# A token-mixing kernel on one core: the filter's way back on quarters of the array, rows exchanged by DMA, six w1 parts made in the first stage and seven low parts by accumulating DMA

## The chip, the cores and the metric

The kernel runs on one core of a Trainium2 chip. The metric is the device time of one execution in microseconds (us); before the change the median of three runs is 391.92 us (391.39 to 392.2). A core has several engines that each work through a queue of their own, in order, and wait for one another through semaphores: TensorE (in the profile PE, its loading of stationary operands PEld), VectorE (DVE), ScalarE (ACT) and GpSimd (POOL). SyncE (SP) computes nothing here; it issues transfers. Sixteen DMA engines carry what SP and POOL issue. Operands lie in SBUF, 128 partitions (rows) wide; TensorE writes to PSUM, which has eight banks, each 512 fp32 columns wide.

## The reference

The input `x` is (1, 2048, 512). Two branches start from its layer norm and meet in a product:

```python
xn = _layernorm(x, axis=-1)
X = rfft2(xn) * (w_r + 1j * w_i)
s = irfft2(X, s=(2048, 512))
h = _layernorm(xn, axis=-1)
u = gelu(einsum("bsd,sf->bdf", h, w1) + b1)
y = einsum("bdf,fs->bds", u, w2) + b2
return x + s * silu(y.transpose(0, 2, 1))
```

`w1` is 2048 x 1792, `w2` is 1792 x 2048. The first branch is a filter in the two-dimensional spectrum, the second an MLP over the tokens.

## The kernel before

The 2048 tokens lie as 128 partitions times 16 blocks `j`. The 1792 hidden features are 14 tiles of 128 (`ft`). Large products run in fp32r with both operands split into a high and a low part, as three matmuls into one bank (`mm3`, lines 121 to 124). The transforms run in plain fp32; the trace shows two matmul records and two weight loads for each such matmul.

**First stage.** For each block `j`: layer norm, seven hidden tiles accumulated in banks 0 to 6 (`hidden_early`, line 333), the first transform of the spectrum into bank 7 (line 212), a copy and a fold into the tile `ey`. The raw `w1` parts of a block are split into high (`high`, ACT, line 325) and low (`low`, DVE, line 328). ACT and DVE instructions of this stage are kept in program order.

**Filter stage.** Two things run interleaved. One is the other seven hidden tiles for all 16 blocks, 112 calls of `hidden` (through `mm3`, so the trace shows them at lines 122 to 124). Their `w1` is fetched in 32 parts, 16 of four tiles each (512 columns, two SP transfers) and 16 of three tiles (384 columns), and split by `w1_part`, three parts ahead; high by ACT, low by DVE, both at line 119. The other is the filter, eight pairs `n` of `filter_pair`:

1. two blocks of four full-array matmuls (line 446), each copied from PSUM to `sh` by ACT;
2. eight matmuls of 64 rows x 32 columns (line 455), two signal halves into banks 5 and 4;
3. for each of two items (`filtered`): ACT makes `zt`, the signal with its upper and lower 64 partitions exchanged (lines 475 and 476); DVE forms sums and differences (lines 484 to 487), multiplies with the weights `wt` (line 493), adds (494), and forms `pq` (498) and `r` (499); ACT brings `r` into `pq` with exchanged halves (503 and 504);
4. the way back: four full-array matmuls an item, `pq` against the constant `hf`, into bank 3 (line 525), copied to `ey` by ACT (line 527).

In between come the gelus (`gelu`, ACT) and the forms of `u` that the last stage needs (`forms`, line 273 and 292 to 295, ACT and DVE). They need tiles of a pool of 25, of which 16 hold the normed input and come free as the hidden tiles pass. A loop over `steps` writes out the order of the filter's steps and paces the hidden tiles evenly between them; a scheduler then orders each engine's instructions for itself.

**Last stage.** Eight pairs of output blocks: `w2` loaded, combined and split (lines 633 to 645), seven products for each pair (line 766), the channel transform (line 701) and the gate. Its first weights share memory with the filter's tiles, which are given back at the end of the filter stage.

Of the kernel before, what the change touches and what calls it, by code (L numbers as in the profile page):

```python
# [22 lines left out]
NS = 25  # L23
WARM = 16
TAIL = 2
# [18 lines left out]
def _constants():  # L44
# [27 lines left out]

    g = np.zeros((P, 8, 2, 2, 32))
    back = np.zeros((8, 2, P, P))
    freq = np.zeros((P, 8, 2), int)
    j = np.arange(16)
    for lo in range(16):
        for hi in range(4):
            k1, (n, l), (t, h) = 16 * hi + lo, divmod(lo, 2), divmod(hi, 2)
            for r in range(16):  # L80
# [7 lines left out]
                elif r == 0:  # L88
                    k = [0, S // 2]
                    out[0, cr], out[1, cr] = 1.0, np.cos(np.pi * j)  # L90
                else:
                    k = [128 * r if r < 8 else 64 + 128 * (r - 8)] * 2
                    th = 2 * np.pi * ((j * k[0]) % S) / S
                    out[0, rows[r >= 8]], out[1, rows[r >= 8]] = np.cos(th), -np.sin(th)
                for s in range(2):
                    p, rows = 64 * s + l * 32 + h * 16 + r, slice(64 * t, 64 * t + 64)
                    g[rows, n, l, s, h * 16 + r] = back[n, t, p, l * 64:l * 64 + 64] = out[s, rows]
                    freq[p, n, t] = k[s]
# [7 lines left out]
        "c_h": back.reshape(16, P, P).astype(np.float32),  # L106
    }
    return c, freq


def spectral_mixer_kernel(tc, x, w1, b1, w2, b2, wk, we, wx, c_f, c_ft, c_d, c_i, c_g, c_h, out):
# [14 lines left out]
    with tc.tile_pool(name="ps", bufs=1, space=PSUM) as psp, ExitStack() as left, ExitStack() as right:  # L126
# [7 lines left out]
        pad = pers.tile([P, 1], F32, name="pad")  # L134
        G.memset(pad, 0.0)
# [4 lines left out]
        hup = pool(left, "left", "hu", NS)  # L140

        def new_hu(name):
            return hup.tile([P, 2, D], F32R, name=name, tag="hu")
# [131 lines left out]
        def held_tile(name):  # L275
            held[0] += 1
            return new_hu(name)
# [26 lines left out]
        def form_parts(n, i):  # L304
            t, k = form[i][n]
            return t[:, k, :D // 2], t[:, k, D // 2:]

# [57 lines left out]
        for j in range(NJ):  # L365
# [3 lines left out]
            if j == 0:  # L369
# [3 lines left out]
                SY.dma_start(b2t, b2)  # L373
            if j == 4:
# [36 lines left out]
            if more:  # L411
                low(w[1][1], raws[j + 1, 1], w[1][0])
                if not early:
# [6 lines left out]
            folds = fold(j, first_copy(j, z))  # L420
        run(folds)
# [10 lines left out]
        G.tensor_sub(e2[:, :, 1], wet[:, :, 1, 1, 1], wet[:, :, 0, 1, 1])  # L432

# [3 lines left out]
        def filter_pair(n):  # L437
# [4 lines left out]
            sh = []  # L442
            for l in range(2):
                pd = ps[:, 6]
# [3 lines left out]
                A.activation(sh[l], pd, AF.Copy)  # L448
                yield

            for s in range(2):
                for l in range(2):
                    for t in range(2):
                        rows, to = slice(64 * t, 64 * t + 64), 64 * s + 32 * l
                        T.matmul(ps[to:to + 32, (5, 4)[t]], gf[rows, l, s], sh[l][rows], start=True, stop=True)  # L455
            items = [filtered(n, t) for t in range(2)]
            for t in (0, 1, 0):
                next(items[t])
            yield
# [5 lines left out]

        def filtered(n, t):

            i = lo = 2 * n + t
            wt = mp.tile([P, 4, 256], F32, name=f"wt{i}", tag="wt")
            SY.dma_start(wt, wk[:, i])  # L470
            hf = mp.tile([P, P], F32, name=f"hf{i}", tag="hf", bufs=3)
            SY.dma_start(hf, c_h[i])
            px = ps[:, (5, 4)[t]]
            zt = mp.tile([P, D], F32, name=f"zi{lo}", tag="zi")
            A.activation(zt[:64], px[64:], AF.Copy, scale=-1.0)
            A.activation(zt[64:], px[:64], AF.Copy)

            def parts(a):
                v = a.rearrange("p (g s c) -> p s g c", s=2, c=64)
                return v[:, 0], v[:, 1]  # L480

            (pr, pi), (tr, ti) = parts(px), parts(zt)
            xc = mp.tile([P, 4, 4, 64], F32, name=f"xc{lo}", tag="xc")
            V.tensor_add(xc[:, 0], pr, ti)
# [3 lines left out]
            s1 = mp.tile([P, 2, 2], F32, name=f"s1_{lo}", tag="s1")  # L488
# [339 lines left out]
```

## Time and profile before

| what | before |
|---|---|
| median of three runs | 391.92 us |
| the profiled execution, its own time | 391.48 us |
| its span, first to last instruction | 389.7 us |
| mean granted TensorE clock | 0.999 |
| first stage | 0 to 98.44 us |
| filter stage | 98.44 to 217.29 us |
| last stage | 217.29 to 389.7 us |
| w1 loads in the filter stage | 36 of 128 KB, 16 of 64 KB, on SP |
| weights of the filter, wt | 16 of 512 KB, on SP |

The stage borders are the start of the first matmul of line 122 and of line 766. In lists of groups the columns are: line, engine, operation, operands, shapes and count, then busy time and mean duration of one (ns), then idle time of that engine just before, with what ended it. Timeline rows give start, duration and operation, with the idle time before in brackets. In the chain of work each piece counts from the point at which the one before it let it go, so pieces add up. A matmul's recorded duration includes the way through the array, so that neighbours overlap; the distance from start to start tells what one costs.

### The profile page before, as it was taken

Reading aid. Unit: us, or ns where it says so; the run is one execution under the profiler, and the core shown is the slowest. Engines: PE = TensorE matmul, PEld = TensorE weight load, DVE = VectorE, ACT = ScalarE, POOL = GpSimd, SP = SyncE. Lnnn points to the kernel's source line nnn. Section 1 sums busy time; section 2 is a strip of 40 time slices with the busy share of each in tenths; the row PEclk is TensorE's granted clock in tenths of the full one; section 3 lists DMA queues with packets and bytes.
Section 4 is the critical chain, followed back from the end, with each engine's and each line's share of the span. In section 5 each row is a group of like instructions: output and inputs, shape, how many; then the busy total and the mean of one; then the engine's idle time right before and its main releaser. Section 6 shows DMA issues by size and latency. Waiting matters only on the chain.

```text
span 389.7 us, 7277 instructions
## 1 busy us (share of the span) xinstructions
PE 380.7 (98%) x2552; PEld 333.8 (86%) x2552; DVE 325.8 (84%) x776; ACT 247.3 (63%) x455; POOL 58.2 (15%) x108
## 2 busy tenths in 40 slices
PE   8999999999999999999989989999999999999995
PEld 4888888888778777887778989999999999999995
DVE  5899998866599999978998699797978788787874
ACT  4676765664878864688748595565656464656442
POOL 2133332321100000000000002120202011110200
PEclk9999999999999999999999999999999999999999
DMA  8957457213725546545617659888868788695602
GB/s 264 325 162 249 136 190 256 69 50 90 218 72 157 170 128 202 150 116 172 195 42 254 135 181 224 197 205 172 227 135 227 148 219 164 197 153 170 110 7 54
DMA packets 33929, 64.21 MB, mean 165 GB/s; under 512 B 4066, under 2 KB 18274, under 8 KB 33764
## 3 DMA queue, kind: packets, MB, share of 16 engines
q1 hardware_dynamic: 29284, 52.33, 42.2%
q0 software_dynamic: 4608, 11.41, 17.7%
q8 instruction: 20, 0.33, 0.3%
q14 instruction: 17, 0.14, 0.1%
HBM read 59.53 MB, written 8.13 MB: 174 GB/s over the span
## 4 chain that ended last, share of the span: by engine, by line
PE 77%; DVE 7%; DMA 7%; ACT 5%; issue 3%; SPq 1%; POOL 0%; DVEq 0%; ACTq 0%; POOLq 0%
PE ps L766 27%; PE ps L333 20%; PE ps L123 5%; PE ps L122 5%; PE ps L124 5%; PE ps L212 4%; PE ps L446 4%; DMA s<-in_w_dram 3%; PE ps L701 3%; PE ps L525 2%; PE ps L455 2%; DMA out_dram<-g 2%; PE ps L322 2%; DVE w2f L645 1%; DMA a<-in_w_dram 1%
## 5 line engine op out<-in xcount | busy, mean ns | idle before, releaser
L333 PE MATMUL ps<-h,w1h 128*128 128x512 f32 x224 | 58.5, 398 | 0.0
L645 DVE TENSOR_TENSOR w2f<-s,w2f 128x896 fp32r<-128x896 f32 x32 | 34.9, 1092 | 18.8 <-ACT w2f L644 18.0
L333 PEld LDWEIGHTS ps<-h,w1h 128*128 128x128 f32 x224 | 40.9, 188 | 7.9
L122 PE MATMUL ps<-h,w1h 128*128 128x512 f32 x112 | 47.1, 422 | 0.0
L124 PE MATMUL ps<-h,w1l 128*128 128x512 f32 x112 | 44.1, 394 | 0.0
L123 PE MATMUL ps<-h,w1h 128*128 128x512 f32 x112 | 43.9, 392 | 0.0
L766 PE MATMUL ps<-fa,w2f 128*128 128x256 f32 x336 | 43.3, 282 | 0.0
L766 PE MATMUL ps<-fc,w2f 128*128 128x256 f32 x336 | 41.7, 280 | 1.1 <-DVE fc L273 1.1
L766 PE MATMUL ps<-fb,w2f 128*128 128x256 f32 x336 | 42.6, 281 | 0.1
L766 PEld LDWEIGHTS ps<-fa,w2f 128*128 128x128 f32 x336 | 41.4, 188 | 0.9 <-DVE w2f L645 0.2
L766 PEld LDWEIGHTS ps<-fc,w2f 128*128 128x128 f32 x336 | 40.2, 188 | 1.7 <-DVE fc L273 1.5
L766 PEld LDWEIGHTS ps<-fb,w2f 128*128 128x128 f32 x336 | 40.7, 188 | 0.7 <-DVE c L736 0.5
L644 ACT ACTIVATE w2f<-s 128x896 fp32r<-128x896 f32 x32 | 30.1, 948 | 16.4 <-DVE s L658 11.3
L635 POOL DMA_DIRECT2D s<-in_w_dram x16 | 13.8, 862 | 120.3 <-DVE tt L709 52.6
L645 DVE TENSOR_TENSOR w2f<-a,w2f 128x896 fp32r<-128x896 f32 x24 | 26.0, 1085 | 5.6 <-ACT w2f L644 5.6
L333 PE MATMUL ps<-h,w1l 128*128 128x512 f32 x112 | 30.6, 390 | 0.0
L122 PEld LDWEIGHTS ps<-h,w1h 128*128 128x128 f32 x112 | 21.2, 189 | 9.9 <-issue 6.7
L644 ACT ACTIVATE w2f<-a 128x896 fp32r<-128x896 f32 x24 | 22.8, 948 | 10.6 <-PE ps L766 7.4
L124 PEld LDWEIGHTS ps<-h,w1l 128*128 128x128 f32 x112 | 21.0, 188 | 4.9 <-DVE w1l L119 0.2
L333 PEld LDWEIGHTS ps<-h,w1l 128*128 128x128 f32 x112 | 21.0, 188 | 4.5
L123 PEld LDWEIGHTS ps<-h,w1h 128*128 128x128 f32 x112 | 21.2, 189 | 3.1
L217 ACT ACTIVATE zt<-ps 128x512 f32<-128x512 f32 x16 | 9.6, 597 | 21.6 <-PE ps L212 21.4
(125 smaller groups left out, 784.1 us busy)
## 6 DMA issues: line engine op xcount, KB each, us to landing
a<-in_w_dram SPq DMA_DIRECT2D x24, 448.0 KB, 3.6
wt<-in_wk_dram SPq DMA_DIRECT2D x16, 512.0 KB, 3.7
s<-in_w_dram SPq DMA_DIRECT2D x16, 448.0 KB, 4.3
s<-in_w_dram POOLq DMA_DIRECT2D x16, 448.0 KB, 6.6
w1s<-in_w_dram SPq DMA_DIRECT2D x48, 128.0 KB, 2.6
w1r<-in_w_dram SPq DMA_DIRECT2D x16, 256.0 KB, 3.6
x<-in_x_dram SPq DMA_DIRECT2D x15, 256.0 KB, 3.3
out_dram<-in_x_dram SPq DMA_DIRECT2D x4, 960.0 KB, 6.6
```

What stands on the lines that cost most here:

```text
L122: T.matmul(o, lh, rh, start=first, stop=False)
L123: T.matmul(o, lh, rl, start=False, stop=False)
L124: T.matmul(o, ll, rh, start=False, stop=last)
L212: T.matmul(z[:, b], h[:, b * P:(b + 1) * P], c, start=True, stop=True)
L217: keep(A.activation(zt, z, AF.Copy))
L333: T.matmul(ps[:, bank + i], w[wi][:, i * P:(i + 1) * P], hj, start=first and j == 0, stop=last and j == NJ - 1)
L446: T.matmul(pd[:, b * P:(b + 1) * P], eyl(2 * n + l)[:, b], cd[:, b], start=True, stop=True)
L635: G.dma_start(t, w2_half(*added), accum_op=ALU.add)
L644: A.activation(wf[:, 0], v, AF.Copy)
L645: V.tensor_sub(wf[:, 1], v, wf[:, 0].bitcast(F32))
L701: T.matmul(pe[:, b % 2, b // 2], yt[:, b], ci[:, b], start=True, stop=True)
L766: T.matmul(o, wf[:, wi, i], ui, start=m + a == 0 and n in (1, 2, 5), stop=m == NH - 1 and a == 2, skip_group_check=n in (6, 3, 7, 4))
```

## The change

The way back becomes matmuls of 64 rows by 64 columns: for each pair `n`, item `t`, block `b`, half `l` and signal part `s` one, each on the quarter (`l`, `s`) of the array, with 64 moving columns, into banks 3 and 4. The signal parts of one frequency now lie 32 partitions apart within a half, and `zt` is no longer made by two ACT copies: ACT makes one copy `px`, and four SP transfers of 32 partitions each exchange its rows into `zt`. DVE forms sums and differences in two operations with a sign taken from the column `turn`, and `pq` comes straight from two more. The real rows of the first item take their weights by four small POOL transfers. The loads `wt` go from SP to POOL's queue.

The first six `w1` parts are loaded, and split by ACT and DVE, in blocks 6 to 11 of the first stage, into six of nine early tiles of the same 25. Of the other 26 parts, seven (10, 12, ... 22) get their low part from an ACT copy with negative sign, to which two POOL transfers add `w1`. Three gelus move ahead of the filter stage. The order of filter steps, form steps and hidden tiles is written out in `PACE`, `MADE` and `LAST`; step 6 of a pair, the way back, stands directly ahead of the forward block of the pair two later. TensorE's instructions of this stage are kept in program order.

```diff
+NV = 9
+NE = 6
+FIRST = 6
+START = 4
+PACE = [(2, 2, 2, 1, 1, 1)] * 4 + [(2, 2, 2, 2, 1, 1)] * 4
+LAST = (4, 4, 4, 4, 4)
+MADE = (3, 3, 3, 3, 3, 3, 2, 2)
+ADDED = range(10, 24, 2)
...
+        def w1_runs(i, where, queue, **how):
+            f = 0
+            for f0, nf in BATCHES[i // NJ][0]:
+                queue.dma_start(where[:, f:f + nf * P], w1[:, i % NJ, f0 * P:(f0 + nf) * P], **how)
+                f += nf * P
+
+        def w1_early_load(i):
+            if i % 2 == 0:
+                pairs[i // 2] = usp.tile([P, 2, D], F32, name=f"w1e{i}", tag="u")
+            w1_runs(i, pairs[i // 2][:, i % 2], SY)
...
+            if FIRST <= j + 1 < FIRST + NE:
+                w1_early_load(j + 1 - FIRST)
...
+                if FIRST <= j < FIRST + NE:
+                    i = j - FIRST
+                    w1_early[i] = new_hu(f"w1e{i}", True)
+                    high(w1_early[i][:, 0], pairs[i // 2][:, i % 2])
+                    low(w1_early[i][:, 1], pairs[i // 2][:, i % 2], w1_early[i][:, 0])
...
+            if i in ADDED:
+                A.activation(wh, w, AF.Copy)
+                A.activation(wl, wh.bitcast(F32), AF.Copy, scale=-1.0)
+                w1_runs(i, wl, G, accum_op=ALU.add)
+                return wh, wl
+            split(wh, wl, w)
...
+        T = Kept(T, keep)
+        w1_parts = [w1_part(0)]
+        for ft, bank in ((2, 2), (0, 0), (1, 1)):
+            next(folds)
+            gelu(ft, bank)
...
-                pd = ps[:, 6]
+                pd = ps[:, 6 - l]
...
-                        rows, to = slice(64 * t, 64 * t + 64), 64 * s + 32 * l
-                        T.matmul(ps[to:to + 32, (5, 4)[t]], gf[rows, l, s], sh[l][rows], start=True, stop=True)
+                        rows, to = slice(64 * t, 64 * t + 64), 64 * l + 32 * s
+                        T.matmul(ps[to:to + 32, 6 - t], gf[rows, l, s], sh[l][rows], start=True, stop=True)
...
+            po = [ps[:, bank].rearrange("p (b t c) -> p b t c", b=4, t=2) for bank in (3, 4)]
+            for t, (pq, hf) in enumerate(((pq0, hf0), (pq1, hf1))):
+                for b in range(4):
+                    for s in range(2):
+                        for l in range(2):
+                            rows = slice(64 * l, 64 * l + 64)
+                            T.matmul(po[l][64 * s:64 * s + 64, b, t], pq[rows, b, s], hf[rows, s], start=True, stop=True)
+            for l in range(2):
+                A.activation(eyl(2 * n + l), po[l].rearrange("p b t c -> p b (t c)"), AF.Copy)
...
-            SY.dma_start(wt, wk[:, i])
+            G.dma_start(wt, wk[:, i])
+            yield
+            px = mp.tile([P, 2, 256], F32, name=f"px{i}", tag="px", bufs=3)
+            A.activation(px[:, ::-1].rearrange("p s (g c) -> p g s c", c=64),
+                         ps[:, 6 - t].rearrange("p (g s c) -> p g s c", s=2, c=64), AF.Copy)
...
+            for to, of in ((0, 32), (32, 0), (64, 96), (96, 64)):
+                SY.dma_start(zt[to:to + 32], px[of:of + 32])
...
-            A.activation(zt[:64], px[64:], AF.Copy, scale=-1.0)
-            A.activation(zt[64:], px[:64], AF.Copy)
...
-            V.tensor_add(xc[:, 0], pr, ti)
-            V.tensor_sub(xc[:, 1], pr, ti)
-            V.tensor_sub(xc[:, 2], tr, pi)
-            V.scalar_tensor_tensor(xc[:, 3], tr, -1.0, pi, op0=ALU.mult, op1=ALU.subtract)
...
+            for k, to in enumerate((xv[:, 0::3], zt)):
+                V.scalar_tensor_tensor(to, zt, turn[:, k:k + 1], px[:, ::-1], op0=ALU.mult, op1=ALU.add)
             V.tensor_mul(xv, xv, wt)
-            V.tensor_add(xv[:, 0:2], xv[:, 0:2], xv[:, 2:4])
+            V.tensor_sub(xv[:, 0:2], xv[:, 0:2], xv[:, 2:4])
...
-            A.activation(pq[:64, :, 1], r[64:], AF.Copy)
-            A.activation(pq[64:, :, 1], r[:64], AF.Copy, scale=-1.0)
...
-                T.matmul(po[:, b], pq[:, b].rearrange("p s c -> p (s c)"), hf, start=True, stop=True)
...
+        for n in range(8):
+            a, b, c, d, e, f = PACE[n]
+            u, v, w = ([None] * (k < MADE[n]) for k in range(3))
+            advance([(n - 1, 5)] * (n > 0) + [(n, 1), a] + u + [(n, 2)] + [(n + 1, 0)] * (n < 7) + [b])
+            advance([(n - 2, 6)] * (n > 1) + [(n, 3), c] + v + [d, (n, 4), e] + w + [f])
+        advance([(7, 5), LAST[0], (6, 6), *LAST[1:], (7, 6)])
```

In `advance` a number stands for so many hidden tiles, `None` for a step of the forms, and `(n, k)` for step `k` of pair `n`: 1 and 2 are the blocks of line 446, 3 the forward block with the exchange, 4 and 5 DVE's work on the two items.

More of the change, by code (lines that the diff above doesn't have):

```diff
@@ L133, in spectral_mixer_kernel @@
         b2t = pers.tile([P, NJ], F32, name="b2t")
-        pad = pers.tile([P, 1], F32, name="pad")
-        G.memset(pad, 0.0)
+        turn = pers.tile([P, 2], F32, name="turn")
+        for row in range(0, P, 32):
+            sign = 1.0 if row % 64 else -1.0
+            G.memset(turn[row:row + 32, 0:1], sign)
+            G.memset(turn[row:row + 32, 1:2], -sign)
         e1 = pers.tile([P, 16, 2], F32, name="e1")
@@ L420, in spectral_mixer_kernel, with w1_part @@
             folds = fold(j, first_copy(j, z))
+        def w1_part(i):
+            if i < NE:
+                return w1_early[i][:, 0], w1_early[i][:, 1]
+            j, (runs, _) = i % NJ, BATCHES[i // NJ]
+            n = sum(r[1] for r in runs) * P
+            w = w1p.tile([P, 4 * P], F32, name=f"w1s{runs[0][0]}_{j}", tag="w1r", bufs=3)[:, :n]
+            w1_runs(i, w, SY)
+            wh, wl = (w1p.tile([P, 4 * P], F32R, name=f"w1{c}{runs[0][0]}_{j}", tag="w1" + c)[:, :n] for c in "hl")
+            if i in ADDED:
[4 more added lines that the diff above has]
+            split(wh, wl, w)
+            return wh, wl
+        T = Kept(T, keep)
[3 more added lines that the diff above has]
+            gelu(ft, bank)
         run(folds)
@@ L441, in filter_pair @@
             yield
-            sh = []
+            sh, items = [], [filtered(n, t) for t in range(2)]
             for l in range(2):
-                pd = ps[:, 6]
+                pd = ps[:, 6 - l]
                 for b in range(4):
@@ L472, in filtered @@
[L472 to L483, printed above, removed]
@@ L552, in spectral_mixer_kernel @@
+            yield pq, hf
+        passed = [NV - NE]
         todo = []
+        late = []
         def form_step():
-            while todo and held[0] + 2 <= NS - NJ + passed[0]:
+            while late:
+                gelu(*late.pop())
+            while todo and held[0] + 2 <= passed[0]:
                 if next(todo[0], "end") != "end":
@@ L598, in spectral_mixer_kernel, with advance @@
         rest = hidden_rest()
[L599 to L603 removed]
+        def advance(work):
+            for what in work:
+                if what is None:
+                    form_step()
+                elif isinstance(what, int):
+                    for _ in range(what):
+                        next(rest)
+                else:
+                    next(chain[what[0]])
         next(chain[0])
[L605 to L606 removed]
+        gelu(9, 6)
         todo.extend(forms(i) for i in FORMS[:3])
         waiting = [[(3, 3)]]
[L609 to L620 removed]
+        advance([START])
+        gelu(8, 5)
+        gelu(7, 4)
+        for n in range(8):
[4 more added lines that the diff above has]
+        advance([(7, 5), LAST[0], (6, 6), *LAST[1:], (7, 6)])
         rstage.close()
+        V, A, T = nc.vector, nc.scalar, nc.tensor
         w2p = pool(right, "right", "w2", 3)
```

172 lines of the change are left out of this document (73 added, 99 removed).

## The prediction

> **What bounds the kernel now.** I read the head of the page first, then the stretches by stage, then the chain of work, then the timeline of TensorE.
>
> ```profile
> span 389.7 us, 7277 instructions
> PE 380.7 (98%) x2552; PEld 333.8 (86%) x2552; DVE 325.8 (84%) x776; ACT 247.3 (63%) x455; POOL 58.2 (15%) x108
> ...
> PE 77%; DVE 7%; DMA 7%; ACT 5%; issue 3%; SPq 1%; POOL 0%; DVEq 0%; ACTq 0%; POOLq 0%
> ```
>
> ```profile
> 0.00:98.44 98.44, 97.08 (x480) 79.75 (x481) 81.14 (x242) 61.60 (x126) 26.99 (x57) 1.00 0.54 179
> 98.44:217.29 118.85, 116.92 (x721) 91.99 (x720) 105.24 (x262) 85.33 (x163) 6.23 (x22) 1.00 0.52 156
> 217.29:389.70 172.41, 166.72 (x1353) 162.03 (x1351) 139.36 (x272) 100.34 (x167) 24.95 (x29) 1.00 0.69 162
> ```
>
> The columns are the stretch, its length, busy time of PE, weight loads, DVE, ACT and POOL, the granted clock (1.00) and the DMA share. Nearly all of the change lies in the second stretch, the filter stage: 118.85 us, PE busy in 116.92 of them, DVE in 105.24. Three quarters of the chain are PE. So this stage shrinks by what its PE work shrinks, and by the pauses that go; DVE and ACT work taken away is worth only pauses.
>
> What a piece of PE work costs stands in the chain, where nothing is counted twice:
>
> ```profile
> 38.76 4.80 PE ps L333 x21
> ...
> 123.36 0.89 PE ps L525 x8
> ...
> 125.65 0.89 PE ps L446 x8
> ```
>
> One 512-column matmul is 4.80/21 = 0.229 us, so a hidden tile (three) is 0.686. Four full-array fp32 matmuls (two records each) are 0.89 us, 0.111 a record. The forward transform L455 works on eight pieces of the array:
>
> ```profile
> 152.57 0.40 PE L124 MATMUL ps<-h,w1l 128*128 128x512 f32 x1
> 152.90 0.66 PE L455 MATMUL ps<-sh,gf 64*32 64x512 f32 x8
> 153.35 0.64 PE L455 MATMUL ps<-sh,gf 64*32 64x512 f32 x8
> 153.92 0.50 PE L122 MATMUL ps<-h,w1h 128*128 128x512 f32 x1
> 154.25 0.40 PE L123 MATMUL ps<-h,w1h 128*128 128x512 f32 x1
> 152.90 0.18 PEld L455 LDWEIGHTS ps<-sh,gf 64*32 64x32 f32 x16 [0.36 <-issue]
> ```
>
> From the start of L124 to that of L123 are 1.68 us; less two matmuls, the block costs 1.22. Eight matmuls side by side take 0.45 a pass, 0.90 for the two, which leaves 0.32 for emptying the array on the way in and out and an uncovered weight load. All 16 weight loads fall in 0.18 us, those of the second pass beside the first pass of the same piece.
>
> The stage now: 112 hidden tiles x 0.686 = 76.8; 16 blocks of L446 x 0.89 = 14.2; 16 of the way back, L525, 14.2; 8 of L455 x 1.22 = 9.8; together 115.0. The other 3.8 us are pauses, the two largest ahead of the way back:
>
> ```profile
> 117.63 0.39 PE L124 MATMUL ps<-h,w1l 128*128 128x512 f32 x1
> 118.54 0.71 PE L525 MATMUL ps<-hf,pq 128*128 128x128 f32 x4 [0.52 <-ACT pq L504]
> 200.82 0.39 PE L124 MATMUL ps<-h,w1l 128*128 128x512 f32 x1
> 202.37 1.16 PE L525 MATMUL ps<-hf,pq 128*128 128x128 f32 x8 [1.16 <-ACT pq L504]
> ```
>
> Start to start 0.91 and 1.55, less 0.23 each: 0.7 and 1.3, 2.0 us in all.
>
> **The change part by part.**
>
> **Way back in quarters.** Removed: 16 x 0.89 = 14.2 us. Added: per pair 32 matmuls of 64x64 with 64 moving columns, 64 records, 16 on each quarter, since the loop rotates through the four. No row shows such a shape. Half the columns of L525 in load and stream give half of its 0.111, 0.056 a record; L455's 0.45 for 512 columns gives 0.056 for 64 as well. With the quarters side by side, as L455's pieces are: 16 x 0.056 = 0.90 us a pair. That is the lower end too, since the stream alone takes it. From above: if a quarter hides none of its load, or its two passes block the next matmul, 0.111 x 16 = 1.78 a pair; if the quarters take turns, 64 x 0.056 = 3.6. I take 0.90, nearest to L455, whose pieces run beside each other now.
>
> Emptying the array comes on top. For six of the eight pairs the way back stands directly ahead of the forward block of a later pair, so that one entry and exit (0.32) serves both, with half of it (0.16, an estimate) between two shapes; two forward and two way-back blocks stand alone. Sum: 2 x 1.22 + 6 x (0.32 + 0.16 + 0.90 + 0.90) + 2 x (0.32 + 0.90) = 2.4 + 13.7 + 2.4 = 18.5, where 9.8 + 14.2 = 24.0 stood: **5.5 us less** (with 1.78 it is 25.6, 1.6 more than now).
>
> **DVE and ACT in the filter.**
>
> ```profile
> L493 DVE TENSOR_TENSOR xc<-xc,wt 128x1024 f32<-128x1024 f32 x16 | 19.1, 1216 | 0.0
> L494 DVE TENSOR_TENSOR xc<-xc 128x512 f32<-128x512 f32 x16 | 10.6, 684 | 0.0
> L119 DVE TENSOR_TENSOR w1l<-w1s,w1h 128x512 fp32r<-128x512 f32 x13 | 8.8, 687 | 0.2 <-ACT w1h L119 0.2
> L119 DVE TENSOR_TENSOR w1l<-w1s,w1h 128x384 fp32r<-128x384 f32 x16 | 8.8, 552 | 0.0
> L484 DVE TENSOR_TENSOR xc<-ps,zi 128x256 f32<-128x256 f32 x16 | 6.7, 420 | 5.5 <-ACT zi L476 5.4
> ...
> L448 ACT ACTIVATE sh<-ps 128x512 f32<-128x512 f32 x16 | 9.5, 595 | 3.2 <-PE ps L455 3.1
> L475 ACT ACTIVATE zi<-ps 64x512 f32<-64x512 f32 x16 | 9.5, 594 | 0.4
> L503 ACT ACTIVATE pq<-r 64x256 f32<-64x256 f32 x16 | 6.7, 416 | 9.9 <-DVE r L502 9.7
> ```
>
> DVE: four quarter-width operations (0.42) become two of 128x512 (as L494, 0.68): 16 x 0.3 = 4.8 us less; of the 13 and 16 low parts in this stretch 7 and 12 stay, six being made earlier and seven by DMA, 6 x 0.69 + 4 x 0.55 = 6.3 less. About 11 of 105 us; the few-column operations balance. ACT: two half-height copies become one (as L448), and the two L503-like copies go: 16 x (0.59 + 0.83) = 22.7 less; seven negated copies come (3 x 0.63 + 4 x 0.52, about 4) and three high parts leave (1.9). Neither engine sets the end, so these 11 and 20 us bring nothing but pauses: the 2.0 us ahead of L525 go, because the copies it waited for are gone.
>
> **Rows exchanged by DMA, weights on POOL's queue.**
>
> ```profile
> 100.91 0.43 SPq L470 DMA_DIRECT2D wt<-in_wk_dram  x1
> ...
> w1s<-in_w_dram SPq DMA_DIRECT2D x16, 64.0 KB, 2.5
> out_dram<-g POOLq DMA_DIRECT2D x15, 256.0 KB, 4.6
> s<-in_w_dram POOLq DMA_DIRECT2D x16, 448.0 KB, 6.6
> L635 POOL DMA_DIRECT2D s<-in_w_dram x16 | 13.8, 862 | 120.3 <-DVE tt L709 52.6 <-DMA s<-in_w_dram 32.9 <-DMA a<-in_w_dram 18.3
> SPq L470 <- DVE xc L493: 19.0, 8, 6.5
> ```
>
> Eight 64 KB exchanges a pair enter SP, 8 x 0.43 = 3.4 us of its time, two wt loads leave it. With gf, two hf and five to six w1 loads, SP issues some 17 a pair, 7.3 us of a period of nine hidden tiles and 4.1 us of filter blocks (two of L446, one double), about 10.2. Behind an exchange that waits for ACT's copy stand hf, gf and w1 loads; w1 has three parts of lead. The chain from the forward block: copies 0.6 to 1.2, four to eight issues 1.7 to 3.4, landing 2.5: 5 to 7 us; then DVE's two halves, each 1.22 + 3 x 0.68 + 2 x 0.42 = 4.1, so 13 to 15 in all. The way back comes two pairs later: 18 hidden tiles (12.3), four blocks of L446 (3.6) and a double block (2.3) after the forward block, 18 us. I cost the exchange at nothing: the hidden tiles cover it; with cover gone each us late is a us of PE, as the order of PE is pinned.
>
> **Low parts by accumulating DMA.** Per part: two ACT copies (1.3), two issues on POOL (1.7), landing 4.6: 7.6 us (9.6 with 6.6). The lead is three parts: some 13 us in the first batch (12 hidden tiles and their filter blocks); 9 x 0.686 plus 0.9 of a pair's 4.1, about 9.8, in the second, where four of the seven lie. New on POOL, wt loads stand ahead of them, and these wait for DVE's multiply: today, on SP, 19.0 us in 8 waits, 2.4 each, 6.5 the longest. 7.6 + 2.4 just fills 9.8, so I take 0.3 us for each of four parts: 1.2.
>
> **Six parts made in the first stage.**
>
> ```profile
> 44.45:50.14 5.69, 5.69 (x30) 4.84 (x30) 5.61 (x15) 3.47 (x7) 1.54 (x3) 1.00 0.38 127
> 50.14:55.83 5.69, 5.69 (x30) 4.84 (x30) 5.44 (x21) 3.56 (x8) 2.28 (x4) 1.00 0.61 194
> ...
> 47.86 0.84 DVE L328 TENSOR_TENSOR w1l<-w1r,w1h 128x512 fp32r<-128x512 f32 x1
> 53.86 1.07 PE L333 MATMUL ps<-h,w1l 128*128 128x512 f32 x4
> ```
>
> A block is 5.69 us of PE, DVE busy 5.4 to 5.6 of it; another 0.69 overfills it by 0.4 to 0.6 in the first two or three blocks, until the statistics end. But DVE ends its low part at 48.7 and PE uses it at 53.9: 5.2 us ahead, against at most 6 x 0.6 = 3.6 lost. ACT is idle two of 5.69, and six loads of 256 KB meet a DMA share of 0.4 to 0.6. I take nothing; without that lead it would be up to 3.6.
>
> **Sum.** 76.8 + 14.2 + 18.5 + pauses 3.8 - 2.0 + 1.2 = 3.0: 112.5, that is 6.3 less than 118.85. The rest stays, the idle at the head of the last stage too:
>
> ```profile
> 219.93 0.50 PE L766 MATMUL ps<-fd,w2f 128*128 128x256 f32 x2 [0.23 <-DVE fd L273]
> 225.09 0.63 PE L766 MATMUL ps<-fc,w2f 128*128 128x256 f32 x3 [0.23 <-DVE fc L273]
> 226.63 0.50 PE L766 MATMUL ps<-fc,w2f 128*128 128x256 f32 x2 [0.91 <-DVE fc L273]
> ```
>
> The profiled execution took 391.48 us, 1.8 around its span; less 6.3 is 385.2. The median of the three runs is 0.4 above the profiled one, so I say **385.5**.
>
> **The rivals.**
>
> Order inside the array. If records start strictly in order, a matmul's second pass holds the next quarter back, each matmul costs 0.056 of the whole array, 32 make 1.78 a pair as now, and the emptying is added: 25.6 for 24.0, pauses as forecast, 7.1 more than the forecast, 392.6. Against it: L455's eight first passes all start ahead of any second. For it: that is 16 records, not 64. The Trainium skill, "TensorE: Matmul & The Clock Gate", Part 3, says that matmuls start and end strictly in program order, and Part 1 that starts are never closer than about 25 ns; the latter would give an estimated 64 x 0.025 = 1.6 a pair. The trace contradicts the second for short bursts (eight records start within one row of 0.66 us); on the first it shows only the order just told.
>
> Low parts late (the slower side). If the wait of wt on DVE is longer, or landing is 6.6, a part is 2.2 us late (9.6 + 2.4 - 9.8), four parts 8.8 where 1.2 was taken: 393. It decides from 1.9 us a part (0.3 plus 6.4/4). For: the 6.5 us wait. Against: DVE carries 11 us less, so the multiply comes sooner.
>
> Quarters take turns: 3.6 a pair, 21.6 more, 407. Against it L455 again.
>
> More is won: all 3.0 us of pauses go and half of the 1.4 at the head of the last stage: 381.5 to 382.
>
> **How the numbers follow.** Forecast, 383 to 389: 0.55. Order inside the array, 391 to 393.5: 0.14. Low parts late, 390 to 397: 0.13. Turns: 0.05. More won: 0.13. The range, 381 to 393, leaves out the turns, half of the late case and the edges. A measurement tells about 0.2%, 0.8 us, from no change: faster 0.73 (forecast, more won, a part of the late case and of the order's low end), same 0.09, slower 0.18.
>
> **What would show it.** Right: the way back's 512 records in some 8 us busy, a pair's 64 within about 1 us, L455-like starts of four at once; the stage ends near 211; L446 and hidden blocks unchanged. Wrong: start to start near 28 ns or 56 ns in the way back; pauses ahead of the third matmul of a hidden tile put down to a POOL DMA; pauses ahead of the way back put down to DVE; blocks of the first stage over 5.69.

## The result, and the profile after

| what | before | after |
|---|---|---|
| median, with the number of runs | 391.92 us (5) | 388.80 us (5) |
| lowest to highest | 391.06 to 393.02 us | 388.18 to 389.64 us |
| the profiled execution, its own time | 391.48 us | 389.61 us |
| mean granted clock in it | 0.999 | 0.991 |

The ratio of after to before is 0.9923, with a 95% interval of 0.9896 to 0.995: 3.1 us faster by the medians, inside the predicted range of 381 to 393, but just under half of the 6.4 us forecast. A second series of the same kernel gave 0.9952 (0.9932 to 0.9973), about 1.9 us.

The stretches of the kernel after the change, first the filter stage, then the stages ahead of and behind it (columns as in the prediction):

```profile
98.02:214.89 116.87, 113.58 (x1106) 88.61 (x1104) 99.17 (x214) 62.99 (x117) 25.87 (x40) 0.97 0.75 196
0.00:98.02 98.02, 96.02 (x480) 79.48 (x481) 84.57 (x248) 65.76 (x132) 27.39 (x64) 1.00 0.61 196
214.89:387.80 172.91, 166.27 (x1353) 161.99 (x1351) 139.52 (x273) 99.42 (x165) 25.16 (x29) 1.00 0.70 161
```

The first stage is no longer than it was (98.44) although VectorE does 3.4 us more in it; the last stage took 0.5 us more (172.41 before). The filter stage went from 118.85 to 116.87 where 112.5 was forecast, and its granted clock is 0.97.

Two places of TensorE's timeline tell the good and the bad part. The first is a way back with the forward block behind it (start, duration, operation; all of this stage now stands under line 132):

```profile
123.44 0.39 PE L132 MATMUL ps<-h,w1l 128*128 128x512 f32 x1
123.75 1.16 PE L132 MATMUL ps<-hf,xc 64*64 64x64 f32 x64
124.85 1.09 PE L132 MATMUL ps<-sh,gf 64*32 64x512 f32 x16
125.87 0.73 PE L132 MATMUL ps<-h,w1h 128*128 128x512 f32 x2
126.44 0.39 PE L132 MATMUL ps<-h,w1l 128*128 128x512 f32 x1
```

From the `h,w1l` at 123.44 to the next at 126.44 are 3.00 us; three hidden matmuls of 0.229 come off, and 2.31 us remain for both tiled blocks. The forecast was 2.28. From the first of the 64 records of the way back to the start of the forward block are 1.10 us. Record by record, the trace has them in groups of four that start some 7 ns apart, a group every 58 ns.

The second place is w1 part 22, the last of the seven whose low part an accumulating DMA makes:

```profile
185.16 0.61 PE L132 MATMUL ps<-h,w1h 128*128 128x512 f32 x2
188.44 0.47 PE L132 MATMUL ps<-h,w1l 128*128 128x512 f32 x1 [2.67 <-DMA w1l<-in_w_dram]
...
190.00 0.80 PE L132 MATMUL ps<-h,w1l 128*128 128x512 f32 x1 [0.62 <-DMA w1l<-in_w_dram]
190.72 1.99 PE L132 MATMUL ps<-hf,xc 64*64 64x64 f32 x64
...
194.08 1.05 PE L132 MATMUL ps<-h,w1h 128*128 128x512 f32 x2
...
195.36 1.04 PE L132 MATMUL ps<-h,w1h 128*128 128x512 f32 x2
```

TensorE has the high part and waits for the low one: it pauses 2.8 us ahead of 188.44 (3.28 from 185.16, less the two matmuls that start there), and again ahead of 190.00. Then the clock falls: the hidden tile at 194.08 takes 1.28 us to the start of the next, 0.427 a matmul where 0.229 is usual. In stretches:

```profile
180.00:190.00 10.00, 6.71 (x30) 4.90 (x28) 9.60 (x22) 2.36 (x6) 2.86 (x4) 0.97 0.90 233
...
190.00:197.00 7.00, 7.00 (x77) 5.55 (x78) 7.00 (x15) 3.39 (x8) 0.00 (x0) 0.55 0.46 118
```

7.00 us at a clock of 0.55 lose some 3.1 us. The trace has the clock at one half from 189.44 to 196.27 us, 6.83 us, which is 3.4 us lost. Pause and clock together are over 6 us. VectorE is busy in all of the 7 us behind 190.

Why the part is late stands in POOL's queue, and why POOL is late in VectorE's and SP's (three timelines):

```profile
181.70 0.55 POOL L564 DMA_DIRECT2D wt<-in_wk_dram  x1 [7.21 <-DVE xc L591]
182.28 1.75 POOL L344 DMA_DIRECT2D w1l<-in_w_dram  x2
```

```profile
178.53 0.16 DVE L587 TENSOR_TENSOR s<-xc,e 128x2 f32<-128x2 f32 x1 [3.09 <-DMA xc<-px]
```

```profile
170.72 1.67 SPq L344 DMA_DIRECT2D w1s<-in_w_dram  x2
172.49 4.98 SPq L573 DMA_DIRECT2D xc<-px  x8
```

POOL waits 7.2 us with a `wt` load for VectorE's multiply, and part 22's transfer stands behind it. VectorE's work on that pair began at 178.5, when the exchange had landed, that is, when its data had arrived; VectorE stood idle 3.1 us for it. SP's eight issues take 4.98 us, 0.62 each. The medians from issue to landing:

```profile
xc<-px SPq DMA_DIRECT2D x64, 64.0 KB, 4.1
...
w1l<-in_w_dram POOLq DMA_DIRECT2D x10, 128.0 KB, 5.3
```

The question is, then: is that chain of queues the cause (theory A below), or is VectorE a second bound at the end of the stage, so that some wait stands there whatever the order (theory B)?

### The profile page after: what moved, and what is told of

Its sections match the earlier page's. It is cut to its first block, busy times and chain, and to the rows that moved or that the text cites. A ratio compares the mean times of both kernels' runs of the same rounds, so it can differ in the third digit from the quotient of the medians.

```text
span 387.8 us, 8067 instructions
## 1 busy us (share of the span) xinstructions
PE 375.9 (97%) x2936; PEld 330.1 (85%) x2936; DVE 323.3 (83%) x734; ACT 228.2 (59%) x412; POOL 78.4 (20%) x133
## 4 chain that ended last, share of the span: by engine, by line
PE 82%; DVE 7%; DMA 4%; issue 4%; ACT 1%; POOL 1%; DVEq 0%; POOLq 0%; ACTq 0%
PE ps L829 27%; PE ps L132 24%; PE ps L377 20%; PE ps L241 4%; PE ps L764 3%; DVE w2f L708 2%; DMA out_dram<-g 2%; DMA w1l<-in_w_dram 2%; PE ps L147 2%; PE ps L366 1%; PE ps L148 1%; PE ps L146 1%; ACT w2f L707 1%; POOL w1l L344 1%; DVE cl L143 0%
## 5 line engine op out<-in xcount | busy, mean ns | idle before, releaser
L377 PE MATMUL ps<-h,w1h 128*128 128x512 f32 x224 | 58.7, 398 | 0.0
L132 PE MATMUL ps<-h,w1h 128*128 128x512 f32 x152 | 50.1, 412 | 0.0
L377 PEld LDWEIGHTS ps<-h,w1h 128*128 128x128 f32 x224 | 40.9, 188 | 7.9
L132 PEld LDWEIGHTS ps<-h,w1h 128*128 128x128 f32 x152 | 28.0, 194 | 10.2 <-issue 5.0
L132 PE MATMUL ps<-h,w1l 128*128 128x512 f32 x76 | 30.7, 403 | 3.3 <-DMA w1l<-in_w_dram 3.3
L377 PE MATMUL ps<-h,w1l 128*128 128x512 f32 x112 | 30.6, 390 | 0.0
L377 PEld LDWEIGHTS ps<-h,w1l 128*128 128x128 f32 x112 | 21.0, 188 | 4.5
L590 DVE SCALAR_TENSOR_TENSOR xc<-xc,turn,px 128x512 f32<-128x512 f32 x32 | 23.9, 747 | 0.0
L372 DVE TENSOR_TENSOR w1l<-w1r,w1h 128x512 fp32r<-128x512 f32 (+1 forms) x32 | 20.7, 648 | 2.4 <-ACT w1h L369 2.2
L805 POOL DMA_DIRECT2D out_dram<-g x15 | 13.4, 896 | 42.3 <-DVE g L803 42.3
L795 ACT ACTIVATE g<-c,b2t 128x256 f32<-128x256 f32 x24 | 12.1, 505 | 15.6 <-DVE c L799 13.1
```

The lines of the kernel that those rows point to most:

```text
L132: return lambda *args, **kw: self.keep(operation(*args, **kw))
L372: keep(V.tensor_sub(dst, src, hi.bitcast(F32)))
L377: T.matmul(ps[:, bank + i], w[wi][:, i * P:(i + 1) * P], hj, start=first and j == 0, stop=last and j == NJ - 1)
L590: V.scalar_tensor_tensor(to, zt, turn[:, k:k + 1], px[:, ::-1], op0=ALU.mult, op1=ALU.add)
L795: A.activation(g[:, cols], src, AF.Silu, bias=b2t[:, j:j + 1], scale=scale)
L805: G.dma_start(out[:, j, cols], g[:, cols], accum_op=ALU.add)
```

## The experiments

Each is the kernel after the change with the edit shown, timed in five rounds beside the kernel before; `us` is the median. Runs of different series are compared by their ratio to before. Where an expectation names a rival, that is the outcome expected if the theory is wrong.

**The same kernel again**, without an edit.

> The changed kernel once more, beside the others. If the pause before w1 part 22 and the clock drop behind it belong to the kernel and not to one execution, they stand in this profile too: a pause of 2 to 4 us at about 185 us, then matmuls of 0.43 us from start to start for some 5 us; about 389 us.

389.33 us, ratio 0.9952 (0.9932 to 0.9973). The same pause of 2.8 us stands ahead of the same part (`187.95`, waiting for the same DMA), but the clock falls less: the filter stage lasts 114.61 us at 0.99, against 116.87 at 0.97. The trace has the clock at one half for 3.41 us here and for 6.83 us there. So some 2 us of the first profile are the clock's, and vary from execution to execution.

**Six low parts by DMA, not seven**, so that VectorE makes part 22.

```diff
-ADDED = range(10, 24, 2)
+ADDED = range(10, 22, 2)
```

> Part 22 gets its low part from DVE again, the other six by DMA. Theory (one late low part stops PE, and the idle array then loses clock): pause and slow stretch go, the granted clock is back at 0.999, the filter stage is about 110.5 us and the time 382.5 to 384. Rival (the exchange and DVE are late in themselves): the pause moves to the way back or to another part and the time stays at 386.5 to 389.

388.66 us, 0.9932 (0.9908 to 0.9957): no gain that a measurement can tell. TensorE's timeline, its two pauses:

```profile
189.09 0.79 PE L132 MATMUL ps<-hf,xc 64*64 64x64 f32 x32 [0.78 <-DVE xc L598]
199.31 0.50 PE L132 MATMUL ps<-h,w1l 128*128 128x512 f32 x1 [1.92 <-DVE w1l L143]
```

The wait for the DMA is gone and two waits for VectorE have come. The clock stayed at 1.00, and still the stage takes 114.15 us.

**No low part by DMA.**

```diff
-ADDED = range(10, 24, 2)
+ADDED = ()
```

> All seven low parts from DVE (some 4.4 us more of DVE work in the filter stage), no accumulating DMA there. Theory (PE bounds the stage, DVE has room): no pause, 382.5 to 384.5, within 0.5 us of the run with six. Rival (DVE is the second bound, and the accumulating DMA buys time): pauses before low parts or the way back, 385 to 389.

392.18 us, 1.0025 (1.0004 to 1.0047): the whole gain is gone, which is more than the rival expected. VectorE is busy 102.5 us of this stage, 3.3 more, and TensorE waits longer for it in the way back:

```profile
193.93 0.79 PE L132 MATMUL ps<-hf,xc 64*64 64x64 f32 x32 [2.20 <-DVE xc L598]
204.16 0.50 PE L132 MATMUL ps<-h,w1l 128*128 128x512 f32 x1 [1.95 <-DVE w1l L143]
```

The seven accumulating DMAs together are worth 3 us or more. That this is VectorE's relief is read from these waits; the edit also takes copies from ACT and transfers from POOL.

**All `wt` loads on SP**, as before the change.

```diff
-            G.dma_start(wt, wk[:, i])
+            SY.dma_start(wt, wk[:, i])
```

> The filter weights wt are issued by SP again, the seven low parts stay on POOL. Theory (the accumulating DMA waited behind wt in POOL's order): part 22's transfers start some 4 us earlier and the pause goes, 383 to 386. Rival (SP now waits for DVE's multiply and holds the exchanges back, so pauses come before the way back): 387 to 393.

397.98 us, 1.0165 (1.0136 to 1.0194): slower than before. SP's waits in the filter stage:

```profile
SPq L564 <- DVE xc L591: 9.9, 5, 2.6
```

Now SP waits for VectorE's multiply (9.9 us in five waits), with exchanges and w1 loads behind it. POOL's queue was the right one for `wt`.

**The seven parts six places earlier**, so that the last two are VectorE's.

```diff
-ADDED = range(10, 24, 2)
+ADDED = range(6, 20, 2)
```

> Seven parts are still made by an accumulating DMA, but parts 6 to 18 instead of 10 to 22; parts 20 and 22 go back to DVE. Theory A (the lost time is one late part: the 2.8 us pause ahead of part 22 and the clock that it costs): the pause goes, 382.5 to 385.5 us, ratio to before .977 to .985. Theory B (VectorE's chain is a second bound at the end of the filter stage, so the wait turns up again, at parts 20 and 22 made by DVE or in the way back): 387 to 390.5 us, and the profile shows pauses of 2 to 3 us behind 180 us that wait for DVE.

389.26 us, 0.9939 (0.9917 to 0.996). The DMA's pause is gone, and TensorE's timeline has another, inside a way back:

```profile
189.33 0.79 PE L132 MATMUL ps<-hf,xc 64*64 64x64 f32 x32 [1.65 <-DVE xc L598]
199.55 0.50 PE L132 MATMUL ps<-h,w1l 128*128 128x512 f32 x1 [0.34 <-DVE w1l L143]
```

The stage takes 114.90 us, of which 1.7 are the clock's (one half for 3.41 us). Theory B holds against theory A: the pause of the DMA is gone, and the gain that theory A expected did not come.

**The pause filled**, with matmuls of zeros ahead of part 22.

```diff
+                    if i == 22 and k == 0:
+                        for _ in range(FILL):
+                            T.matmul(ps[:, bank, :P], nil, nil, start=False, stop=False)
```

> The kernel after the change with 44 matmuls of zeros (128 bf16 columns each, some 2.4 us together) put on TensorE ahead of part 22's first group, so that the array works where it paused; they add zeros and change no result. Theory (the fall of the granted clock behind the pause is worth time of its own): the clock stays near 1.0 behind part 22 and the kernel comes out at 386 to 388.5 us, .5 to 3 us below the kernel after the change. Rival (the pause alone counts, the clock follows something else): no gain, 388.5 to 390.5 us, and the granted clock still falls behind 190 us.

392.14 us, 1.0015 (0.9996 to 1.0033): by the ratios 2.5 us or more slower than the kernel without them, and outside both expected ranges. The 44 take 2.44 us from start to start, and the profile shows no fall of the clock in any stretch behind them:

```profile
186.52 2.63 PE L133 MATMUL ps<-nil 128*128 128x128 bf16 x44
188.96 0.72 PE L133 MATMUL ps<-h,w1h 128*128 128x512 f32 x2
...
200.43 0.50 PE L133 MATMUL ps<-h,w1l 128*128 128x512 f32 x1 [1.23 <-DVE w1l L144]
```

But a wait of 1.2 us for VectorE follows, and the profiled stage, 115.21 us, is no shorter than those above. The profiled run was 1.5 us longer in the first stage and 0.9 in the last than `same_again`, stages that the edit does not touch; why is not settled. So the clock did not fall where the pause was filled, in this one profile; the gain was not there.

**The way back apart from the forward block.**

```diff
-            advance([(n - 2, 6)] * (n > 1) + [(n, 3), c] + v + [d, (n, 4), e] + w + [f])
+            advance([(n, 3), c] + v + [(n - 2, 6)] * (n > 1) + [d, (n, 4), e] + w + [f])
```

> The way back of a pair is moved some four groups later in the order, so that it no longer stands beside the forward block of a later pair: six tiled blocks more are entered and left. By the sum of the prediction (.32 us for a pair of entry and exit, .16 between two tiled shapes) this costs 6 x .16 to 6 x .32, 1 to 2 us: 389.5 to 391.5 us. Rival (the later place gives VectorE's chain more time and takes waits ahead of the way back away, where there are any): the same or faster, 386.5 to 389 us.

392.54 us, 1.0027 (1.0003 to 1.005). Forward blocks in TensorE's timeline, in a stretch without pauses, first of this kernel, then of the unedited one (`same_again`):

```profile
124.02 1.09 PE L132 MATMUL ps<-sh,gf 64*32 64x512 f32 x16
134.51 1.09 PE L132 MATMUL ps<-sh,gf 64*32 64x512 f32 x16
```

```profile
124.62 1.09 PE L132 MATMUL ps<-sh,gf 64*32 64x512 f32 x16
134.88 1.09 PE L132 MATMUL ps<-sh,gf 64*32 64x512 f32 x16
```

A pair's period is 10.49 us instead of 10.26: an entry and exit more costs 0.23, in the middle of the 0.16 to 0.32 of the sum, 1.4 us for six. The rest of the 3 to 4 us by the ratios is only in part accounted for: a pause of 0.69 us for ACT's copy `sh`, at 180.5, is new, and the one for part 22's DMA is about as long as without the edit (2.45 us, at 191.5; 2.39 there).

**No part made in the first stage.**

```diff
-NE = 6
+NE = 0
```

> No part of w1 is made in the first stage; six more are made by ACT and DVE at the start of the filter stage, .69 us of DVE and .51 us of ACT each, some 4 us of DVE. Theory B (DVE is a second bound in the filter stage): 390.5 to 394 us, with waits of TensorE for DVE. Rival (the early parts buy nothing, since DVE has slack early in the stage): 388 to 390 us.

390.63 us, 0.9987 (0.997 to 1.0004): 1.4 to 2.5 us slower than with them, by the ratios. VectorE is busy 102.4 us of the filter stage, and the pause ahead of part 22 is the longest of all:

```profile
190.95 0.47 PE L132 MATMUL ps<-h,w1l 128*128 128x512 f32 x1 [3.54 <-DMA w1l<-in_w_dram]
```

It is a wait for a DMA, but the DMA's issue waits on POOL, and POOL waits 7.1 us for VectorE's multiply, ahead of which VectorE itself stood idle 3.0 us for the exchange. The time is in theory B's range. Its interval touches that of `same_again`, so the gain of the early parts is small and only just clear of the noise.

**The last pair's `wt` on SP.**

```diff
-            G.dma_start(wt, wk[:, i])
+            (G if i < 14 else SY).dma_start(wt, wk[:, i])
```

> Only the two wt loads of the last pair (items 14 and 15) go back to SP's queue, so that the accumulating DMA of w1 part 22 no longer stands behind the 7.2 us that POOL waits there for VectorE. Theory A (POOL's order makes part 22 late): its DMA is issued some 4 us earlier, near 178 us instead of 182.3, the 2.8 us pause ahead of part 22 goes, and with it the fall of the clock. If nothing else is as late, 383 to 385.5 us; theory B (VectorE's chain is as late at the end of the stage): the pause of part 22 goes, another of 1.5 to 3 us for VectorE stands in the way back or ahead of a low part behind it, 386.5 to 389 us. Rival (SP, waiting for VectorE in its turn, holds up exchanges or w1 loads): 389.5 to 392 us.

389.62 us, 0.9957 (0.9935 to 0.9978), which lies just inside the rival's range, with an interval that reaches into theory B's; the waits are those of theory B. POOL's transfer for part 22 went out 2.8 us earlier than in the first profile, and TensorE waited elsewhere (POOL's timeline, then TensorE's):

```profile
179.46 1.74 POOL L344 DMA_DIRECT2D w1l<-in_w_dram  x2 [3.92 <-ACT w1l L484]
```

```profile
189.35 0.79 PE L132 MATMUL ps<-hf,xc 64*64 64x64 f32 x32 [0.95 <-DVE xc L598]
199.67 0.50 PE L132 MATMUL ps<-h,w1l 128*128 128x512 f32 x1 [2.05 <-DVE w1l L143]
```

No pause for a DMA is left, the clock is 1.00, and the stage takes 114.52 us: the order of POOL's queue alone is not what sets its length.

**Two kernels with one form step fewer beside the seventh pair**, this one and that of `added_ahead`.

```diff
-MADE = (3, 3, 3, 3, 3, 3, 2, 2)
+MADE = (3, 3, 3, 3, 3, 3, 1, 2)
```

> Both at once: the two wt loads of the last pair on SP, and one form step of GELU (six instructions of VectorE, some 2.4 us) made behind the stage's last pair instead of beside the pair before it. Theory B (VectorE's chain is the second bound at the end of the stage): the wait that takes the place of part 22's pause shrinks by as much, 384 to 387 us, and below last_wt_on_sp by 1 to 2.4 us. Rival (VectorE is not what is late, or the step is as late at the stage's end): within 1 us of last_wt_on_sp, or slower.

> The kernel of added_ahead (parts 6 to 18 by accumulating DMA), with the same form step moved behind the last pair. Its pause of 1.86 us in the way back at 187.5 us stood for VectorE. Theory B: that pause shrinks to under .5 us and nothing takes its place, 386 to 387.5 us, some 2 us below added_ahead. Rival (the wait only moves, to the low parts behind 195 us or to the head of the last stage, which needs the forms): 388.5 to 390.5 us.

390.12 us, 0.9961 (0.9942 to 0.9979), and 388.77 us, 0.9931 (0.9912 to 0.995): each within 0.5 us of its parent. These two decide nothing. The order of VectorE's instructions in them is that of their parents, so the permission that `MADE` gives was not what held the form step there. They serve as a repetition, and show that 0.5 us is not a difference.

**Less work for VectorE**, nothing moved. These two kernels leave out a subtraction for six items, so that their output is another one; they measure and are no versions to use.

```diff
-            V.tensor_sub(xv[:, 0:2], xv[:, 0:2], xv[:, 2:4])
+            if i < 10:
+                V.tensor_sub(xv[:, 0:2], xv[:, 0:2], xv[:, 2:4])
```

> The kernel after the change without the subtraction of line 592 (128x512, .69 us of VectorE) for the items of the last three pairs, 10 to 15: 4.1 us of VectorE less, nothing moved, no instruction of another engine changed; the values of the filter's way back are then other ones. Theory B (VectorE is the second bound at the end of the filter stage): part 22's DMA, which waits on POOL for VectorE's multiply, is issued 2 to 3 us earlier and the pauses behind 180 us shrink by 2 to 4 us in sum, 384.5 to 387 us, 2 to 4 us below the kernel after the change. Rival (the loads are late by themselves: landing times and the queue's order): within .7 us of it, 388 to 389.5 us.

> The same subtractions left out in the kernel of last_wt_on_sp, where no pause waited for a DMA any more and those at 188 (1.2 us) and 197 (2.2 us) stood for VectorE. Theory B: both go or shrink below .3 us, and the stage loses 2.5 to 3.5 us: 385.5 to 387.5 us, 2 to 3.5 us below last_wt_on_sp. Rival (with one wait gone, TensorE waits for ACT's high part or for a w1 load in its place): 388 to 390 us.

386.29 us, 0.9871 (0.9841 to 0.9901), and 386.02 us, 0.9878 (0.9845 to 0.991). By the ratios that is 2.0 to 3.2 us below the kernel after the change, and 3.1 below `last_wt_on_sp`, for 4.1 us of VectorE's work. The stage by the windows, the one with `wt` as in the change, then the one of `last_wt_on_sp`:

```profile
98.14:209.69 111.55, 110.64 (x1106) 86.60 (x1105) 95.37 (x208) 62.78 (x116) 25.86 (x40) 1.00 0.77 204
```

```profile
98.27:209.78 111.51, 110.95 (x1105) 86.41 (x1104) 95.69 (x208) 62.74 (x116) 24.72 (x38) 1.00 0.76 203
```

111.5 us where every order tried above took 114.2 us or more. In the second, no wait of TensorE for a DMA was there to begin with, and the two for VectorE (0.95 and 2.05) shrank to one of 0.51; the clock was 1.00 in both. So VectorE's work is shown to be the second bound at the end of this stage. The first kernel is the weaker evidence: part 22's transfer went out at 181.55 us, no earlier than in `same_again` (181.49), where 2 to 3 us were expected, since VectorE had stood idle 3.2 us for the exchange ahead of the multiply. The pause shrank from 2.8 to 1.1 us mostly because the transfer landed sooner, for a reason that is not settled, and 1.7 us of the difference to `same_again` in the stage are the clock's.

**A subtraction given to POOL**, on top of `last_wt_on_sp`.

```diff
-            V.tensor_sub(pq[:, :, 1], xc[:, 0], xc[:, 1])
+            G.tensor_sub(pq[:, :, 1], xc[:, 0], xc[:, 1])
```

> A version that may beat both: the kernel of last_wt_on_sp with the subtraction of line 596 (128x256, .42 us on VectorE) given to POOL for all 16 items; POOL's 128x128 additions took .51 to .57 us, so some 1 us each there, beside VectorE's line 595. VectorE has 6.7 us less over the stage and 1.7 us less over the last two pairs. Theory B: 387 to 388.5 us, 1 to 2.5 us below last_wt_on_sp. Rival (each item's own chain gets .6 us longer, and POOL's instructions, which come in order, hold up wt and the accumulating DMAs): 389.5 to 392 us.

391.15 us, 0.9993 (0.9971 to 1.0015): the rival. Groups of POOL, then of VectorE, in this stage:

```profile
L596 POOL TENSOR_TENSOR xc<-xc 128x256 f32<-128x256 f32 x16 | 21.2, 1322 | 23.1 <-DVE xc L592 13.0 <-DMA w1s<-in_w_dram 7.3 <-issue 2.5
```

```profile
L595 DVE TENSOR_TENSOR xc<-xc 128x256 f32<-128x256 f32 x16 | 9.9, 621 | 0.1
```

Line 595 on VectorE, 0.42 us before, takes 0.62 on average beside POOL, so that of the 6.7 us given away 3.2 came back; VectorE's busy time fell by 0.5 us only (99.24 to 98.70). And POOL's in-order queue now put the subtraction, waiting 6.5 us for VectorE, ahead of part 22's transfer, which went out at 185.6 instead of 179.5. TensorE paused 3.0 us for it.

**The exchange on ACT's queue**, for all items, and for the last six (`SY if i < 10 else A`).

```diff
-                SY.dma_start(zt[to:to + 32], px[of:of + 32])
+                A.dma_start(zt[to:to + 32], px[of:of + 32])
```

> All 64 exchanges go into ACT's queue, right behind ACT's own copy into px, instead of SP's, where those of one pair stood behind a w1 load that waited for VectorE's low part (px was ready near 169.8 us, the first exchange was issued at 172.5, and VectorE then stood idle 3.1 us). Theory C (SP's order starves VectorE, and VectorE's backlog then makes the pauses behind 180 us): VectorE's idle time for the exchange falls from 3.1 to under 1 us there and the kernel takes 386 to 388 us. Rival (ACT, which spends .6 us on each issue, some 39 us over the stage, is late with its own copies): 389.5 to 394 us, with waits of TensorE for ACT.

> The same for the items of the last three pairs alone (10 to 15, 24 exchanges, some 14 us of ACT). Theory C: the same gain as exchange_on_act without its cost, 385.5 to 387.5 us, 1.5 to 3 us below the kernel after the change. Rival (VectorE's work, not its idle 3 us, sets the end): 388 to 390 us; ACT late: above 390 us.

401.83 us, 1.0261 (1.0226 to 1.0295), and 392.20 us, 1.0019 (0.9995 to 1.0043): ACT is late, twice, and the first is slower than even the rival expected. Timelines of the second, ACT's, then VectorE's:

```profile
171.52 6.82 ACTq L573 DMA_DIRECT2D xc<-px  x8
178.44 0.52 ACT L483 ACTIVATE w1h<-w1s 128x384 fp32r<-128x384 f32 x1 [6.46 <-DMA xc<-px]
```

```profile
179.84 0.16 DVE L587 TENSOR_TENSOR s<-xc,e 128x2 f32<-128x2 f32 x1 [4.85 <-DMA xc<-px]
```

ACT spends 6.8 us on eight issues, 0.85 each, in which it copies nothing. Behind them stand, after 6.5 us without computing, the high part of a w1 part, its negated copy and its low part. The exchange began 1 us sooner (171.52 for 172.49; 2 us, counted from the start of the stage), but VectorE's idle time for it grew from 3.1 to 4.85 us, and to 4.90 with all items on ACT, where theory C expected under 1. So SP's queue was the better place, and theory C itself was not put to the test: neither kernel took the idle time away.

No version that computes the same was measurably faster than the change itself.

## Why the gain came out half as large as predicted

**The way back in quarters: right.** 2.31 us a joint block for 2.28; with the subtraction left out, where one pause of 1.1 us was left, the stage took 111.55, so TensorE's work is some 110.4 us where the sum had 109.5. Two expected signs were there, a pair's 64 records in 1.10 us and starts of four at once; the 512 records were busy 10.4 us where some 8 were expected. The rivals "order inside the array" (1.78 us a pair) and "quarters take turns" (3.6) are refuted. On the first the Trainium skill's "TensorE: Matmul & The Clock Gate", Part 1, was weighed: by its closest start of about 25 ns, 64 records would take an estimated 1.6 us; the 1.10 us here are 17 ns each, and the measurement decides.

**Early parts at nothing: right** for the first stage: 98.02 us for 98.44, and 97.8 to 99.4 in all profiles of kernels that make them there. That they bring nothing to the filter stage was wrong: without them the kernel is 1.4 to 2.5 us slower by the ratios.

**The exchange at nothing: wrong in its sizes.** An issue took 0.62 us (0.43 taken), landing 4.1 us (2.5 taken). The way back itself was not late in the profiled run of after, but VectorE stood idle 3.1 us ahead of 178.5, so that all its later work, with hardly an idle moment behind it, began later. The same idle time of 1.4 to 3.2 us stands there in the profile of every version with the exchange on SP.

**"Neither engine sets the end, so these 11 and 20 us bring nothing but pauses": the step that failed**, and with it the pauses of 3.0 us. VectorE was set aside because TensorE was busy in 116.92 of 118.85 us. But VectorE was busy in 105.24 of them, and TensorE's work was to shrink to 109.5. A sum for VectorE's share of the last pairs was not made: behind 178 us it has two pairs, several low parts and the forms to finish, and it was busy 9.6 of the ten us from 180 on and all of the seven behind 190. What TensorE saved beyond VectorE's pace came back as pauses. The term for pauses was 3.0 us; the stage's excess over 110.4 was 6.5 us in the profiled run of after (some 3 us pause, the rest the clock), and 3.7 to 5.2 in the seven profiles of kernels that repeated it, moved the wait or filled it. Taking work from VectorE, which the prediction held to be worth only the pauses of before, was worth 3.0 us of the stage for 4.1 us of work (114.52 to 111.51, `less_vector_last_wt` against `last_wt_on_sp`). VectorE's need at the end is its work and its idle time for the exchange; no run took that idle time away by itself, so how much of the loss is the exchange's stays open.

VectorE's relief was also smaller than the 11 us of the sum. Added up by rows its work did fall by about 11 us, but its busy time fell by 6.1 (105.24 to 99.17): neighbouring instructions overlap, as here in the kernel after,

```profile
182.77 0.42 DVE L595 TENSOR_TENSOR xc<-xc 128x256 f32<-128x256 f32 x1
183.11 0.42 DVE L596 TENSOR_TENSOR xc<-xc 128x256 f32<-128x256 f32 x1
183.44 0.75 DVE L590 SCALAR_TENSOR_TENSOR xc<-xc,turn,px 128x512 f32<-128x512 f32 x1
```

0.42 long, but 0.34 from start to start. Two smaller errors of the sum cancelled. The sign-taking operations of line 590 took 0.75 where 0.68 was taken from line 494, 2 us in all. And three of the seven parts made by DMA are of four tiles, so that 4 low parts of 128x512 stayed where the sum had 7, 2 us less.

**"The rest stays, the idle at the head of the last stage too": off as well.** The last stage took 172.91 us in the profile of after, and 172.4 to 175.9 in all seventeen profiles of kernels with the change, 173.9 in the middle; the one profile of before has 172.41. In `same_again` the filter stage is 4.2 us shorter than before and the first stage 0.6, but the last is 1.9 longer (174.29), and 3.0 remain of the span. At the head of the last stage, where TensorE before waited 1.4 us for VectorE's forms `fd` and `fc`, it now waits 1.55 us for the first operands that ACT and VectorE make for that stage, here in the kernel after:

```profile
224.70 0.50 PE L829 MATMUL ps<-fc,w2f 128*128 128x256 f32 x2 [0.30 <-ACT w2f L707]
225.83 2.50 PE L829 MATMUL ps<-fc,w2f 128*128 128x256 f32 x19 [0.62 <-DVE w2f L708]
230.12 0.50 PE L146 MATMUL ps<-ch,cft 128*128 128x512 f32 x1 [0.63 <-ACT ch L143]
```

In `same_again` 0.8 us for `fc` come on top, 2.3 in all; that is 1.0 us more than before and half of the 1.9. No run tested the rest, and with one profile of before it is not settled how much of it is the change's.

**"Low parts late", the slower rival: right in its place, small in its price.** It decides at 1.9 us a part; four parts were feared, one was late, by 2.8 us, because its `wt` load waited 7.2 us (2.4 taken, 6.5 was the longest wait in the trace of before). But it was not the cause alone: with part 22 given to VectorE (`six_added`, `added_ahead`) or the last `wt` loads taken out of that queue (`last_wt_on_sp`) the stage was about as long.

**Left open:** why some executions lose 2 us more to the clock than others; how far an earlier exchange would bring VectorE's start forward; why the last stage is longer. A third buffer for `wt`, which might shorten POOL's wait, was not tried.

## What to carry to other kernels

When the bounding engine's work shrinks, work out every other engine's need in the same stretch, above all in its last part, where no lead is left: the second-busiest engine can set how much of the gain stays. Its need is its work and what it must wait for before it can begin. A wait that moves from one engine to another at each edit, while the stage keeps its length, is a sign of such a second bound; the test is to take a little of that engine's work away and move nothing. Relief is worth only what the helping engine's queue does not hold up in turn.

## What the runs showed of the hardware

After a pause of 2.8 us the granted clock fell to one half (0.427 us a matmul) for 6.83 us; after the same pause in another execution of the same kernel (`same_again`) for 3.41 us, half as long. After shorter pauses it fell or did not: in `added_ahead` it was at one half for 3.41 us behind a pause of 1.65, in `none_added` and `last_wt_on_sp` it did not fall behind pauses of 2.20 and 2.05. The Trainium skill, "TensorE: Matmul & The Clock Gate", Part 1, has the array at half rate after an idle window of about 3.4 us that runs free of the program, so that its effect varies: the half rate and the variation agree with these runs, but here pauses shorter than such a window sufficed, and the measurement decides.

A two-operand addition on VectorE beside POOL's subtraction can take over twice its time. Timelines of VectorE and POOL with the subtraction given to POOL:

```profile
184.94 0.96 DVE L595 TENSOR_TENSOR xc<-xc 128x256 f32<-128x256 f32 x1
...
189.64 0.41 DVE L595 TENSOR_TENSOR xc<-xc 128x256 f32<-128x256 f32 x1
```

```profile
184.43 1.19 POOL L596 TENSOR_TENSOR xc<-xc 128x256 f32<-128x256 f32 x1 [6.53 <-DVE xc L592]
...
189.44 1.53 POOL L596 TENSOR_TENSOR xc<-xc 128x256 f32<-128x256 f32 x1 [2.13 <-issue]
```

In six of the sixteen items the addition took 0.95 to 0.96 us, as in the first row; in the ten others 0.41 to 0.43, although POOL's subtraction is on record at the same time in nearly all of them, as in the second. There POOL's took up to 2.63 us. Spans on POOL are rough in the profile, and which of the two gives way, and why, these rows do not show. The Trainium skill, "GPSIMD Engine Reference", section "Key points", says that POOL shares its SBUF interfaces with VectorE and that they contend when a VectorE instruction has two inputs in SBUF; the longer times beside each other agree with it.
